# Attention, expert layer and gated layer on one core: output's zeros written later, and the whole order of the work replaced

## Chip, cores and metric

The kernel runs on one core of a Trainium2 chip. The metric is the device time of one execution in microseconds (us), lower is better; the time of a kernel is the median over its runs.

## What is computed

Three layers, one after another, over 1152 tokens (2 batches of 576) of 512 columns. The reference, cut to its core:

```python
def _attn_ref(q, k, v, w_phi):
    def phi(x):
        proj = np.einsum('bhsd,df->bhsf', x, w_phi)
        proj = proj - np.max(np.abs(proj), axis=-1, keepdims=True)
        return np.concatenate([np.exp(proj), np.exp(-proj)], axis=-1)
    q_p, k_p = (phi(q), phi(k))
    kv = np.einsum('bhsf,bhsd->bhfd', k_p, v)
    num = np.einsum('bhsf,bhfd->bhsd', q_p, kv)
    den = np.einsum('bhsf,bhf->bhs', q_p, np.sum(k_p, axis=2))[..., None] + 1e-06
    return num / den

def _moe_ref(x, w_gate, w1, w2, capacity):      # 8 experts, capacity 288
    ...                                          # expert_idx, gate_w: top expert of each token
    # the first `capacity` tokens of each expert are its rows disp[e]
    h = np.maximum(np.einsum('ecd,edf->ecf', disp, w1), 0.0)
    y = np.einsum('ecf,efd->ecd', h, w2)
    ...                                          # out[token] = gate_w * y of its row, or 0

def _moe2_ref(x, w_gate, w_val, w_out, rms_g):   # 1536 inner columns
    xn = x / np.sqrt(np.mean(x * x, axis=-1, keepdims=True) + 1e-06) * rms_g
    g = xn @ w_gate
    return (g / (1.0 + np.exp(-g)) * (xn @ w_val)) @ w_out
```

## The kernel before

**Stages.** First the attention (projections L601, sums over keys L674, queries L751, transposes L719), which ends at about 85 us. While it runs, each batch of finished token tiles is routed (argmax of the gate's logits) and its rows are scattered by POOL (L402) into a table `disp` in DRAM, ordered by expert. Then come passes over the experts. A pass takes one expert's rows, 288 at most, out of `disp` by three gathers on POOL (L399: two tiles of 128 rows and one of 32), scales each tile by its gate value on ACT or DVE (L957, L956), transposes it on PE (L964, four groups of three, one for each 128 columns), and multiplies by `w1` and `w2`. The first pass begins while the attention still runs: its rows were scattered early. The second pass needs rows of all tiles, so its first gather waits until the last batch's three scatters have landed in `disp`. The last stage is the gated layer, from whose rows ACT copies each finished set of output out of its PSUM bank (`rows_out`, L1161); POOL then scatters them into `out_y` (five scatters, L402), since the rows stand in expert order. Rows of `out_y` that no scatter reaches must be zero, so `fill_out` (L1387) writes nine blocks of 128 rows of zeros (256 KB each, from the tile `zrow`, L1389), all of which must lie ahead of the first scatter of output.

**Precision.** Every product of weights is done as three matmuls (L974, L975, L976: high x high, high x low, low x high); the high half of a tile is a cast (L417 on DVE or L418 on ACT), the low half a subtraction on DVE (L414, `lower`). Weight tiles `w4` (nine buffers) are loaded by SP from `in_w12` (`load_w`, L917, 512 KB) and, for the gated layer, from `in_gvo` (L534).

**The order.** Every piece of work is recorded by `Sched.op` or `Sched.any` (L113 to L138) with its engine, a cost, and what it reads and writes; `any` gives two ways (such as DVE or ACT). `Q.run(PLAN)` (L1698) then issues them in the order of the table `PLAN` (L34): each of its numbers, in base 36, is a piece of work and the way taken. An engine works through its own list in that order, and a list that meets a wait holds everything behind it. SP's list holds all loads of weights and the zeros; what it waits for there are buffers and registers. The dependency of the zeros on `tick[0]` in L1389 is one of the recording: it says where the table may put them, and adds no wait on the chip.

**Tiles.** `xg` and `b2` tiles serve many uses in turn: token rows on their way to `disp`, gathered rows, high and low halves of weights. A low half that goes into the tile of a scatter has to wait until that scatter has landed.

Of the kernel before, what the change touches and what calls it, by code (L numbers as in the profile page):

```python
# [38 lines left out]
f3 f1 eq co fj cw am cq 9y fk g0 ca gk cu cy di b4 a3 fh d0 go gt a0 cs b8 gu fm bc fp d2 bi ce fs fu dc be gm fq b6 da bk du bg d8 c6 d6 de gw j4 ho dg dp j6
ei e0 gr ba fw f8 hs fy jb f4 1ne hy j8 gy fc e2 fa h0 g4 fe i6 e4 g6 f6 em hx hq g8 jd gc d4 i8 hv ic h2 h4 ie ge ga gi h8 ig im dw iq ha dk lw i2 hc ii nj  # L40
ik ji he gg hg i0 io m0 dq hk e6 dz ek je nk kg mw i4 jk n4 is dm dt iu n6 iy my lg ki iw j0 li m6 k0 ko lk le e8 km lm j2 lq k2 hm jg hi ea m4 ly kl eo l2 k4
lu jm kc kq m2 mu l8 jo 114 o4 l5 kw js lb lo kt ec ju jq mq jw ls ms 158 jy n1 ma k8 l6 ku 110 lc kz g2 l0 o8 mc n2 me n8 oa pm oc mg og ee oe mi ok ke nf eg
mm oo oq ou k6 os qa h6 ow na ka nm oy ng qc nc qe qq qi p4 qs q7 qk pj qm qu 138 170 qo qg no m8 nw mk p6 mo ny qy om nq o6 rs r2 o0 16y qw oi p1 nu 136 ns
r0 pc pe p8 ta pa ru pg p2 rw ry o2 r4 ps t4 r7 pp 16w s0 s2 s4 pu 19s s6 s8 sa sc se q4 q0 py pq r8 uc 1ru q2 th 172 ue ra pk sg pw si ug v2 rp rk rc uz v4
tc sk 112 sm ui rm q8 174 t6 re t2 176 ti 116 v0 uv 18m tf 13a rq yh so ri 18k uk rg us zc uo uw v6 uq ze zu sq tl um t8 yi vk yf vc v8 109 zg zq va ve vu 118
vm 18o vo 14i vq yw vh yk ss z2 yq yz yn vw vi w2 z5 vs yt 10y zz su zs z6 10d w4 vy yo z0 w0 yu wo we 18q 10e 10u 102 100 wg 104 zw 106 wk 18i 11w sw wc 12e
132 11t wu ws sy 13c t0 11u 10s 10a 10g 11y 178 10o 19q to 11b 120 12k 10i 194 14l 153 10k 10q 134 198 196 ww 12h wi 128 10w 13f tq 124 10m wy wm 12a 14m 12m
154 12s tu 11c x0 19u x2 122 1dc 126 13g 12c 12q 12w 12i 18s 19w x4 14f 13x 19y 160 x6 12u 140 12o x8 12z 15c 130 13y 156 xa 14g xc 148 142 14a xe 14c tm 16f
za xg xi 144 15x xk 19a z8 zi xm 162 146 14o 150 wq 1a0 14u 18u 1d0 14w xo 14q 16g tt 15y 1d2 xq 14y 14s w7 zk 19c 164 16i 168 11q 19f w8 y8 1d4 wa 1d6 15a
11o 16a 166 19g 15e xs 16c y2 16s zm 1a5 11e 13s 1d9 1eq 16u 16k 11g 1es 15g xu 16q 16o 16m y4 17m 17k zo 1eu 13m 13u 11i y6 1ew 11l 17g 17i 11m 13i 1am 1ae  # L50
1a2 1ey 1ai xw 13o 15i xy 13q ya 1f2 1eo 15m 1aa 1as y0 1aq 1au 1a6 13k 1da 15q 15s 1aw 1ao 15o 1dy tw 1ay yc 1hk 17a 17c 1f0 1b0 15u 1b2 1b4 1b6 1b8 1ag 17e
1ba 1f4 18w 1cy 17o 1f6 1bc 1be 1bg 1bi 1cu 1bk 15k 17q 1a8 1e2 1ac 1f8 1hi 17s 1bm 17u 17w 1ak 1fa 17y 1fd 1bu 180 1hc 1c0 1c2 182 184 186 1de 1hm 1cw 18y
1o4 188 1e4 1bo 1ho 1c4 18a ty 18c 18e 1bq 1lw 1c6 1ek 1hg 1e6 18g 1e8 1fe 1dg 1di 190 19i 1c8 1cc 1cm 1ca 1bs 19k 1bw 1fo 1ce 1ea 1by 1cq 1ci 1dk 192 19m 1dn
1he 1cg 1hq 1ga 1dq 1me 1mc 1do 1ck 1ec u0 1fs 1em 1cs 1fg 19o 1mg 1ok 1gc 1ee 1co 1hs 1ei 1ds 1ge 1fu 1fw 1gq 1mi u2 1iw 1mk 1om 1hy 1jk 1fy 1jo 1oo 1hw 1dv
1oq 1i0 1gw 1gi 1ku 1dw 1fi 1ot 1ou 1gu 1gk 1gg 1mm 1ks 1g0 1k2 1i2 1g2 1i8 1eg 1io 1hu 1gy 1iq 1h0 1h4 1j2 1fl 1g8 1h6 1h2 1fm 1ia 1g6 1j0 1i5 1i6 1k6 1gn
1im 1n0 1g4 1iy 1l4 1j4 u4 1id 1go 1h8 1k4 1k8 1ha 1ik 1mo 1jq 1js 1jm 1ii 1kg 1j6 1ki 1pk 1ie 1kw 1la 1ju 1l8 1je 1j8 1ig 1ji 1ja 1jg 1ky 1mq 1jw 1kl 1nc 1lc
1jz 1ka 1le 1n2 1ms 1km 1jc 1k0 1lo 1mu 1ma 1lq 1it 1iu 1ow 1ni 1kc 1ls 1ng 1o6 1nk 1ko 1lg 1lj 1ke 1m0 1kq 1p8 1o8 1lm 1oy 1r4 1l0 1oi 1rg 1l2 1nm 1qc 1ny
1p0 1lk 1lu 1oa 1pq 1oc 1ly 1of 1m2 1nr 1mw 1og 1po 1p2 1nu 1n4 1ps 1n6 1m4 1nw 1m6 1tc 1no 1rs 1qu 1qs 1pa 1r6 1my 1qw 1pu 1to 1ri u6 1ry 1n8 1pz 1q8 1m8 1q4
1rw 1ns 1uq 1s0 1na 1q2 1q6 1qg 1te 1qa 1vg 1rk 1s2 1r8 1tq 1p6 1ra 1qq 1qe 1p4 1sc 1s4 u8 1qi 1qy 1se 1vi 1pw 1rm 1so 1sy 1sa 1s7 1vo 1th 1ti 1vq 1ug 1qk 1sk
1q0 1ro 1sm 1r1 1s8 1sq 1o0 1qn 1ss 1uu 1u0 1t0 1vl 1qo 1t2 1vm 1wq 1rq 1su 1uk 1l6 1t4 1us 1sw 1ws 1uw 1w0 1t6 1xa 1sg 1wu 1uy 1r2 1t9 1wy 1ui 1wg 1wk 1w2  # L60
1o2 1v1 1pc 1v2 1v6 1pe 1ta 1wi 1si 1ww 1um 1xu 1ts 1tu 1ph 1pi 1w4 ua 1re 1ys 1tm 1v4 1rc 1xq 1tx 1v8 1u4 1u2 1u6 1y0 1w6 1xs 1x0 1tk 1ze 1va 1w8 1vc 1wa 1y2
1uo 1e0 1vs 1u8 1vu 1ud 1ua 1ue 1xe 1vx 1xc 1ty 1xg 1yu 1fq 1wc 1xi 1vy 1y5 1xm 1wm 1y6 1yi 1xw 1we 1ve 1zg 1y8 1z8 1wo 1x2 1yw 1z6 1xy 1gs 1za 1x4 1x6 1yk
# [1815 lines left out]
```

## Time and profile before

| | |
|---|---|
| time, median of 3 runs | 284.78 us (284.45 to 285.24) |
| the profiled execution's own time | 283.31 us |
| its span | 281.5 us, 7648 instructions |
| mean granted TensorE clock | 0.986 |
| PE busy | 269.8 us, 2993 matmuls |
| DVE, ACT, POOL busy | 209.6, 166.2, 27.8 us |
| moved by DMA | 48.58 MB, mean 173 GB/s |

The span is the stretch from the first to the last instruction of one execution; 1.8 us of the profiled execution's time lie around it. PE is busy nearly throughout, so what matters is the few places where it is not, or where its clock is lower, and what ended last before it went on there.

### The profile page before, as it was taken

What the parts mean: (1) busy time and instruction counts of PE and PEld (TensorE: products, weight loads), DVE (VectorE), ACT (ScalarE), POOL (GpSimd) and SP (SyncE); (2) the same over time, 40 slices, a digit from 0 to 9 for tenths busy, and PEclk for the clock granted to TensorE, in tenths of its full rate; (3) what the DMA queues carried; (4) which work ended last, traced back from release to release, by engine and by line L of the source; (5) the groups of instructions that cost most, each with busy time, mean ns of one, the idle gap of its engine ahead of it and who ended that gap; (6) DMA issues with size and microseconds to landing.
All of it is one profiled execution on the core that took longest, in us unless ns stands there. A gap on an engine that the chain in (4) does not pass through costs nothing.

```text
span 281.5 us, 7648 instructions
## 1 busy us (share of the span) xinstructions
PE 269.8 (96%) x2993; PEld 253.8 (90%) x2993; DVE 209.6 (74%) x583; ACT 166.2 (59%) x370; POOL 27.8 (10%) x62
## 2 busy tenths in 40 slices
PE   8999999999999979999999999999999999999990
PEld 8899999998999869999979999999999999999970
DVE  2988768968898868999999898795974863464330
ACT  2996874999954445876748767456643634231040
POOL 4000000340054400100000000000000000000042
PEclk9999999999999997999999999999999999999996
DMA  5754245499065587788795737655654820141023
GB/s 191 208 139 117 81 140 130 128 371 393 31 206 174 156 323 220 228 252 280 238 322 166 191 104 261 197 186 185 186 151 149 238 100 0 75 151 41 0 78 116
DMA packets 22092, 48.58 MB, mean 173 GB/s; under 512 B 3427, under 2 KB 8547, under 8 KB 22048
## 3 DMA queue, kind: packets, MB, share of 16 engines
q1 hardware_dynamic: 20496, 44.13, 49.6%
q0 software_dynamic: 1552, 3.88, 3.8%
q8 instruction: 25, 0.41, 0.6%
q14 instruction: 19, 0.16, 0.2%
HBM read 39.93 MB, written 9.18 MB: 174 GB/s over the span
## 4 chain that ended last, share of the span: by engine, by line
PE 65%; DVE 9%; issue 9%; ACT 6%; DMA 6%; POOL 2%; SPq 0%; POOLq 0%; DVEq 0%; ACTq 0%
PE bank L976 10%; PE bank L975 10%; PE bank L974 10%; PE bank L674 6%; PE bank L751 5%; PE bank L601 4%; PE bank L979 3%; PE bank L980 3%; PE bank L981 3%; PE bank L719 3%; DMA xg<-disp,at 2%; DMA disp<-xg,rt 2%; POOL out_y L402 2%; ACT k L651 2%; DMA out_y<-zrow 2%
## 5 line engine op out<-in xcount | busy, mean ns | idle before, releaser
L975 PE MATMUL bank<-w,k 128*128 128x384 f32 x96 | 32.5, 338 | 0.1
L976 PE MATMUL bank<-w,k 128*128 128x384 f32 x96 | 32.4, 337 | 0.0
L974 PE MATMUL bank<-w,k 128*128 128x384 f32 x96 | 32.4, 337 | 0.0
L565 ACT ACTIVATE cat<-w 128x512 int32<-128x512 uint8 x36 | 24.1, 675 | 9.4 <-DVE cat L566 4.5
L563 ACT ACTIVATE cat<-w 128x512 f32<-128x512 f32 x36 | 24.1, 672 | 9.4 <-DVE cat L566 3.9
L1145 ACT ACTIVATE h<-bank 128x256 f32<-128x256 f32 (+1 forms) x24 | 10.1, 433 | 32.3 <-PE bank L976 25.5
L615 DVE TENSOR_REDUCE m<-bank 128x4 f32<-128x512 f32 x36 | 23.5, 683 | 7.5 <-PE bank L601 7.4
L566 DVE SCALAR_TENSOR_TENSOR cat<-cat 128x512 int32<-128x512 int32 x36 | 24.7, 688 | 5.5 <-ACT cat L563 5.0
L974 PE MATMUL bank<-ua,k 128*128 128x256 f32 x96 | 27.2, 283 | 0.0
L975 PE MATMUL bank<-ua,k 128*128 128x256 f32 x96 | 27.2, 283 | 0.0
L976 PE MATMUL bank<-ua,k 128*128 128x256 f32 x96 | 27.0, 282 | 0.0
L568 DVE SCALAR_TENSOR_TENSOR cat<-w,cat 128x512 int32<-128x512 int32 x36 | 24.5, 685 | 0.1
L1146 DVE TENSOR_TENSOR h<-h,bank 128x256 f32<-128x256 f32 (+1 forms) x24 | 11.4, 484 | 17.6 <-ACT h L1145 11.8
L651 ACT ACTIVATE k<-b 128x512 f32<-128x512 f32 x36 | 19.8, 629 | 3.0 <-DVE b L627 3.0
L751 PEld LDWEIGHTS bank<-kvt,k 128*64 128x64 f32 x576 | 18.7, 136 | 1.1 <-ACT k L725 0.4
L751 PE MATMUL bank<-kvt,k 128*64 128x73 f32 x576 | 19.4, 227 | 0.3 <-ACT k L725 0.2
L725 ACT ACTIVATE k<-bank 128x512 f32<-128x512 f32 x36 | 18.8, 622 | 0.9 <-PE bank L719 0.9
L632 ACT ACTIVATE b<-bank,m 128x128 f32<-128x128 f32 x56 | 15.9, 413 | 5.2 <-DVE m L615 4.4
L601 PE MATMUL bank<-wph,b 64*128 64x128 f32 x288 | 19.0, 279 | 0.0
L414 DVE TENSOR_TENSOR h<-h,h 128x256 fp32r<-128x256 f32 (+1 forms) x24 | 11.7, 487 | 9.8 <-PE bank L980 6.4
L974 PEld LDWEIGHTS bank<-ua,k 128*128 128x128 f32 x96 | 18.2, 190 | 0.8 <-PE bank L1336 0.4
L975 PEld LDWEIGHTS bank<-w,k 128*128 128x128 f32 x96 | 18.0, 188 | 1.0 <-DVE w L1384 0.4
(263 smaller groups left out, 737.6 us busy)
## 6 DMA issues: line engine op xcount, KB each, us to landing
w<-in_gvo SPq DMA_DIRECT2D x36, 512.0 KB, 4.2
w<-in_w SPq DMA_DIRECT2D x24, 512.0 KB, 5.0
wo<-cat SPq DMA_DIRECT2D x12, 256.0 KB, 3.7
b<-in_v SPq DMA_DIRECT2D x9, 256.0 KB, 3.6
b<-in_qt SPq DMA_DIRECT2D x9, 256.0 KB, 3.4
...
disp<-xg,rt POOLq DMA_INDIRECT x9, 3.9
```

The source lines that it names most:

```text
L563: op("ACT", c_act(512, False), lambda: nc.scalar.activation(out=m.t, in_=hf(), func=AF.Abs, scale=REBASE), [st], [m])
L565: op("ACT", c_act(512, False), lambda: nc.scalar.activation(out=ai(), in_=top(), func=AF.Copy, scale=1.0 / 32, bias=-31.0 / 64), [st], [a])
L566: op("DVE", c_dve(512), lambda: nc.vector.scalar_tensor_tensor(out=ai(), in0=mi(), scalar=3, in1=ai(), op0=ALU.logical_shift_left, op1=ALU ...
L568: op("DVE", c_dve(512), lambda: nc.vector.scalar_tensor_tensor(out=ai(), in0=hi(), scalar=-0x80000000, in1=ai(), op0=ALU.bitwise_and, op1= ...
L601: nc.tensor.matmul(v4(hs[r].t)[:, c, :], lhsT=v4(x.t)[h, c, :], rhs=wph[h, :], start=c == 0, stop=True, skip_group_check=True)
L615: op("dve", c_dve(512), lambda hf=hf: nc.vector.tensor_reduce(out=m.t[:, 4 * hf:4 * hf + 4], in_=v4(hs[hf].t), axis=AX.X, op=ALU.max, appl ...
L651: nc.scalar.activation(out=kv_(sg)[:, hf::2, :], in_=v4(s[hf].t), func=AF.Exp, scale=s[hf].sign * (1.0 - 2 * sg))
L725: nc.scalar.activation(out=q_[:, sg, hf::2, :], in_=v4(p.t), func=AF.Exp, scale=s[hf].sign * (1.0 - 2 * sg))
L751: nc.tensor.matmul(nv(num)[r0:r1, i, :], lhsT=q_[:, c, 2 * i + hf, r0:r1], rhs=kvr[b][:, 2 * i + c, 73 * hf:73 * hf + 73], start=i == 0 an ...
L974: nc.tensor.matmul(o, lhsT=wh, rhs=xs[0], start=fst, stop=False, skip_group_check=True)
L975: nc.tensor.matmul(o, lhsT=wh, rhs=xs[1], start=False, stop=False, skip_group_check=True)
L976: nc.tensor.matmul(o, lhsT=wl, rhs=xs[0], start=False, stop=lst_, skip_group_check=True)
```

## The change

Three edits. First, the zeros' place in the recording: they now depend on the three copies of the second pass's token indices (`idi`, made from each gathered tile as it arrives) instead of on `tick[0]`, so that the table puts all nine behind these gathers.

```diff
     def fill_out(i):
-        dma(lambda: nc.sync.dma_start(out=out[i * P:(i + 1) * P, :], in_=zrow[:, 0:512]), [(V["zrow"], 0), tick[0]], [(V["out"], ("z", i))])
+        dma(lambda: nc.sync.dma_start(out=out[i * P:(i + 1) * P, :], in_=zrow[:, 0:512]), [(V["zrow"], 0), *[(V["idi"], (1, j)) for j in range(3)]], [(V["out"], ("z", i))])
```

Second, the copy of the last set of output rows is no longer split between ACT (288 columns) and DVE (224). Lines behind it move up by three.

```diff
         def rows_out(s, i):
             a, m, idx = sets[s][3][i]
             o, row = oac[s, i], new("b2")
-            e = 512 if (s, i) != (seq[-1][0], len(sets[s][3]) - 1) else 288
-            op("ACT", c_act(e), lambda: nc.scalar.copy(out=row.t[0:m, 0:e], in_=o.t[0:m, 0:e]), [o], [(row, 0)])
-            if e < 512:
-                op("dve", c_dve(512 - e), lambda: nc.vector.tensor_copy(out=row.t[0:m, e:512], in_=o.t[0:m, e:512]), [o], [(row, 1)])
+            op("ACT", c_act(512), lambda: nc.scalar.copy(out=row.t[0:m, 0:512], in_=o.t[0:m, :]), [o], [row])
```

Third, the whole table `PLAN` is another one, so every engine's list stands in another order, and some casts change between DVE and ACT. Its first line and the one in its place:

```diff
-8 0 2 6 u a c 12 e 14 g 16 18 1a m 1o 28 2e 1f o 22 1c i 1s 1g 1i 2i 4 1q 1w 30 1k 1u q w k 3i 2n 34 3g y 2s 32 3m 2u 20 1y 2g 24 10 4k 3e 2k 3q 2q 26 37 4m
+0 o a e 8 2 c g 4 12 14 16 u m 18 i 1c 1o 1a 2e 1h w 28 22 q k 1k 1e 1q 2g 30 s 1s 3i 1i 1w 2l 3g 1u 2i y 20 2u 10 1y 3m 2s 3e 2m 1m 32 34 4k 2a 3q 2q 4m 36
```

PE issues the same 2993 matmuls. At the very start SP now issues two pieces of the first key tile, then the projection weights `wph`, then the tile's last piece, where `wph` came first before. Of the nine blocks of zeros, one stood among the first pass's weights, two at the second pass's gathers and six in the gated layer; now all nine stand in the gated layer's part of SP's list.

What the table moves around the second pass's gathers is seen at three places.

SP's list from the last loads of the first pass to the first of the second (`in_w12` an expert's weights, `in_gvo` the gated layer's, `lst0` the register that holds the second pass's expert). Before:

```order
L917 DMA w4_2_1836<-in_w12 128x1024
L534 DMA w4_1_1905<-in_gvo 128x512
L1389 DMA out_y<-zrow_69 128x512 x2
L1584 TENSOR_LOAD lst0_86
L1584 ISA x2
L917 ISA
L917 DMA w4_3_2055<-in_w12 128x1024
L917 ISA
L917 DMA w4_5_2067<-in_w12 128x1024
```

With the change:

```order
L917 DMA w4_0_1813<-in_w12 128x1024
L534 DMA w4_2_1910<-in_gvo 128x512
L917 ISA
L917 DMA w4_1_1929<-in_w12 128x1024
L1581 TENSOR_LOAD lst0_86
L1581 ISA x2
L917 ISA
L917 DMA w4_4_1960<-in_w12 128x1024
L917 ISA
L917 DMA w4_8_2065<-in_w12 128x1024
```

The two blocks of zeros are gone from here; the last weight tile of the first pass (`w4_1_1929`) stands where they stood, behind the load from `in_gvo` instead of ahead of it.

DVE's list at the low half that goes into the last scatter's tile (`xg_0`), which therefore waits for that scatter. Before:

```order
L414 TENSOR_TENSOR xg_3_1929<-w4_8_1726,b2_5_1901 128x512
L417 CAST b2_6_1931<-w4_0_1749 128x512
L566 SCALAR_TENSOR_TENSOR cat_106<-cat_106 128x512
L414 TENSOR_TENSOR xg_0_1940<-w4_0_1749,b2_6_1931 128x512
L414 TENSOR_TENSOR b2_2_1955<-w4_3_1609,b2_4_1806 128x512
```

With the change, the piece from the low half of `w4_4_1592` on:

```order
L414 TENSOR_TENSOR b2_3_1902<-w4_4_1592,b2_4_1806 128x512
L1484 SCALAR_TENSOR_TENSOR key_88<-cnt_94,off_84 128x9
...
L417 CAST b2_8_1936<-w4_0_1813 128x512
L1517 SCALAR_TENSOR_TENSOR at_98<-place_95,rt1_112 128x3
L417 CAST b2_0_1939<-w4_0_1813 128x512
L414 TENSOR_TENSOR xg_0_1947<-w4_0_1813,b2_8_1936 128x512
L414 TENSOR_TENSOR b2_2_1958<-w4_6_1620,xg_1_1896 128x512
```

Before, the last reader of the weight tile `w4_3_1609`, whose buffer the second pass's first load takes (`w4_3_2055`), stood behind the waiting low half. Now the last reader of `w4_4_1592`, whose buffer `w4_4_1960` takes, stands ahead of it.

PE's list at the second pass's transposes (L964, from the gathered tiles `xg` and `b2`), preceded by matmuls of the first pass. Before:

```order
L974 MATMUL bank_1853<-h_1_1996,xg_2034 128x288
L975 MATMUL bank_1853<-h_5_2062,xg_2034 128x288
L976 MATMUL bank_1853<-h_1_1996,xg_2060 128x288
L964 MATMUL bank_2124<-ident,xg_1937 128x128
L964 MATMUL bank_2124<-ident,b_3_1899 128x128
L964 MATMUL bank_2124<-ident,b_8_1868 128x128
```

With the change:

```order
L974 MATMUL bank_1851<-h_0_2036,b_4_2058 128x288
L975 MATMUL bank_1851<-h_6_2076,b_4_2058 128x288
L976 MATMUL bank_1851<-h_0_2036,b_6_2067 128x288
L964 MATMUL bank_2125<-ident,xg_1815 128x128
...
L964 MATMUL bank_2129<-ident,b_5_2001 128x128
L974 MATMUL bank_1845<-h_2_2099,b_7_2014 128x288
L975 MATMUL bank_1845<-h_7_2137,b_7_2014 128x288
L976 MATMUL bank_1845<-h_2_2099,b_1_2106 128x288
L964 MATMUL bank_2145<-ident,xg_1815 128x128
```

The first transpose was PE's 610th row and is now its 613th, three matmuls later, and three more matmuls now part the second group of transposes from the third. On ACT the scaling of the second gathered tile (L957) stood behind the copy of the third tile's indices (L934 from `xg`); it now stands behind that of its own.

## Rows read from the trace of the kernel before

**Rows 1.** The page's head and first part: busy time, share of the span, instructions.
```profile
span 281.5 us, 7648 instructions
PE 269.8 (96%) x2993; PEld 253.8 (90%) x2993; DVE 209.6 (74%) x583; ACT 166.2 (59%) x370; POOL 27.8 (10%) x62
```

**Rows 2.** Windows; columns: width, each engine's busy time, PEclk granted, DMA share, GB/s.
```profile
93.00:94.00 1.00, 0.49 (x4) 0.44 (x4) 1.00 (x2) 0.00 (x0) 0.33 (x1) 1.00 0.00 0
102.00:103.00 1.00, 0.45 (x4) 0.22 (x2) 0.15 (x1) 0.00 (x0) 0.00 (x0) 1.00 0.97 336
103.00:104.00 1.00, 0.00 (x0) 0.00 (x0) 0.21 (x1) 0.22 (x2) 0.00 (x0) 1.00 1.01 377
104.00:105.00 1.00, 0.68 (x4) 0.49 (x5) 1.00 (x3) 1.00 (x2) 0.00 (x0) 1.00 0.81 324
105.00:106.00 1.00, 0.74 (x7) 0.51 (x5) 1.00 (x3) 1.00 (x4) 0.00 (x0) 1.00 0.17 66
106.00:107.00 1.00, 0.78 (x4) 0.79 (x5) 1.00 (x5) 0.79 (x3) 0.00 (x0) 0.71 0.47 74
107.00:110.00 3.00, 3.00 (x14) 3.00 (x14) 3.00 (x7) 1.49 (x4) 0.00 (x0) 0.53 0.81 254
```

**Rows 3.** Chain of waits from 64 to 112 us; columns: start, us, what.
```profile
87.41 5.29 DMA disp<-xg,rt
92.81 0.70 DVE xg L414
...
94.23 0.13 PE bank L976
...
96.81 6.95 DMA xg<-disp,at
103.79 0.47 DVE xg L956
...
106.23 0.74 PE bank L964 x3
106.98 0.24 PE bank L974
```

**Rows 4.** Timeline of SP's queue; columns: start, us, what was issued, how often.
```profile
87.03 0.34 SPq L534 DMA_DIRECT2D w<-in_gvo  x1
87.41 0.91 SPq L1389 DMA_DIRECT2D out_y<-zrow  x2
94.23 6.59 SPq L917 DMA_DIRECT2D w<-in_w  x5
```

**Rows 5.** Line L402 from 84 to 85.2 us: landing of its one scatter, issued at 84.21.
```profile
DMA to landing us min/median/max: 3.2/3.2/3.2
```

**Rows 6.** Line L399 from 117 to 118 us: landing of its one gather, issued at 117.65.
```profile
DMA to landing us min/median/max: 4.8/4.8/4.8
```

**Rows 7.** Timeline of DVE at the wait for the last scatter.
```profile
92.81 0.69 DVE L414 TENSOR_TENSOR xg<-w,b 128x512 fp32r<-128x512 f32 x1 [2.04 <-DMA disp<-xg,rt]
93.42 0.69 DVE L414 TENSOR_TENSOR b<-w,b 128x512 fp32r<-128x512 f32 x1
```

**Rows 8.** Timelines of SP and PE at the start, and landing of L472's three pieces.
```profile
0.81 0.39 SPq L469 DMA_DIRECT2D wph<-in_wphi  x1
1.25 1.38 SPq L472 DMA_DIRECT2D b<-in_kt  x3
4.60 2.96 PE L601 MATMUL bank<-wph,b 64*128 64x128 f32 x48
DMA to landing us min/median/max: 2.0/2.0/2.2
```

**Rows 9.** Timelines of ACT and POOL at the end: copies of output rows, and last scatter.
```profile
272.42 0.40 ACT L1165 COPY xg<-bank 128x288 f32<-128x288 f32 x1 [2.75 <-DVE xg L1167]
274.77 0.58 ACT L1165 COPY b<-bank 128x512 f32<-128x512 f32 x1 [0.80 <-PE bank L981]
275.65 0.97 POOL L402 DMA_INDIRECT out_y<-b,idi  x1 [0.30 <-ACT b L1165]
```

More of the change, by code (lines that the diff above doesn't have):

```diff
@@ L39 @@
[L39 to L62, printed above, removed]
@@ new lines @@
+8s ac 9d 8y 9e 92 8w 8u es ae 82 9s ag ai 90 7s am ak ao as au 9g ay b0 b2 aq aw 9q bm bo c0 eu bs c2 8k bq bu 84 c8 bw a8 by cg 8m 9u ew ci ck cm co ey eq c4
+9w cc cq 9y fg ca f1 b4 fj f3 cw fl a3 a0 gk fm gu be fp gy g0 fq b8 cs bc du bg ce fs b6 h0 bi ba d8 cu dc go cy f8 fv 6 d0 f4 de c6 da ei dg fw gs gm gw h6
+fy bk g2 i2 do ho j4 dj gr j6 em d2 i6 hs d6 hw fa fc mw e0 f6 hq ic i4 dw i8 g4 hy i0 ji ie hu d4 ig jb ik j8 ek iq e2 jc dk fe g6 my h2 g8 ga e4 jk h4 ii io
+nj lw h8 ha hc je gc kg gi gg hg e6 n5 he dq im hm e8 jg hk ge is lg nk ea dy ki mu li iu ly dn hi iy ko iw m4 lk kl m6 eo j0 ma lm dt j2 kn jm 110 lu k0 m0
@@ new lines @@
+qa lo lq le ec l2 l8 jo m2 js k2 kq kw ju lb mc kz 158 kt k4 n6 jw kc k8 mq jy me lc l0 mg ku l5 ms l6 ls ee o8 mi oa mm oc p1 og oe ok n8 o4 nm oo 112 oq n1
+jq os p2 ou qq pp ow ka oy n2 eg qc no nf k6 qe qi qs qk o1 qm ps qu na qo oi pj 16y ke qg pm th 136 pu om r2 mk 114 m8 qy p4 mo nc o6 ru nw pq nu ra qw nq rw
+ry ny r4 ns p6 s0 r0 ng o2 ud pg 170 pk s2 q7 p8 s4 16w t5 s6 s8 sa pe pw q4 pa sc rs q2 rc r6 se ro pc py r8 t2 ue 10y q0 rk ug 172 rg 116 v2 re tb 138 13a
+q8 um tc 18k vh uy v0 rq sg 18m ri 11t si t6 rm v4 uq ui ti 18o uk uo sk 13c tf us uu va 11u zc uw sm vc v8 v6 zg ze 13f vk yh t9 vm ve yf 18q vi so to tk sq
@@ new lines @@
+vq zr yi vu vs yq z2 12e ss yt vo su 13g w2 yk yw 18t z5 zs yu yn z6 yo 18i w0 yz z0 sw 174 zz vw vy 12a wg w4 100 10d 132 102 118 wk wc wq zv 10e 10g 19q 14i
+zw 11w 104 wo we 176 ws sy wu 106 12c 109 ww 11b 12k 18u 10i 10s 12z 10k 198 11y t0 10o 10a 12h wy 11c 196 x0 178 10v 10q 124 194 134 120 19u 13x 128 14f 10w
+tm 10m tq 126 122 12s 12i 13y 12m 19w x2 130 12q 12o za x4 15c 140 19y 156 1a0 x6 142 14k zk 12u 153 144 148 14m 1d2 12w 14o 154 14q 19a x8 1d0 14c 14a 146
+19c 14w 1d4 15x 1dc 15a 160 xa zi 14s xc tt wi 150 14g 15e z8 162 xe 16e 14u 14y xg 11o 164 16c 15g 166 xi 19f w6 xk 1eq 168 16o 16q xm 1d6 wm 16u 11q w8 xo
@@ new lines @@
+1fs 1fi 1ee 1cc 1cm 1he 1ds 1eg 1bs 1cq 1ce 1lw 1io 1cg 1em 1by 1co 1iq 1ci 1me 1ga 1fw 1ei 1cs 1ck 1fy 1mc 1gy 1jo 1mg u0 1hy 1fl 1g3 1gi 1gc 1mi 1p8 1hw 1ml
+1g4 1i0 1dv 1k4 1dw 1i2 1ik 1mm 1k6 1i4 1fm 1o4 1g8 1ge 1g6 1gk 1k8 1gg 1i8 1om 1iw 1gn 1i6 1go 1h0 1is 1n0 1g0 1ia 1j2 1ha 1h4 1pm 1ok 1iu 1kg 1ka 1h8 1oo
+1j0 1r4 1hu 1qc 1n2 1h6 1h2 1im 1oq 1j4 1ow 1ii 1j6 1kd 1ig 1jq 1ks 1js 1ke 1ic 1ju 1ku 1pa 1jb 1ot 1l8 1ie 1mo 1ne 1jc 1la 1ko 1ou 1je 1nc 1ma 1jw 1j8 1o6
+1iy 1lc 1kq 1ki 1o8 1gs 1k2 1le 1ri 1oi 1mq 1ng 1jm 1oy 1r6 1jy 1kl 1k0 1ji 1mt 1lj 1oa 1jg 1lg 1ni 1oc 1nk 1ls 1kw 1rs 1ru 1km 1ly 1m0 1lm 1lk 1m2 1lo 1lq
@@ new lines @@
+1ky 1qs 1qu 1rg 1qw 1l0 1oe 1e0 1mu 1nm 1lu 1l2 1tc 1m4 1pk 1qy 1mw 1qg 1nu 1m6 1m8 1r8 1my 1p1 1tq 1qe 1te 1qi 1fq 1qk 1sy 1r0 1ny 1nq u2 1r2 1to 1p2 1qn 1q2
+1nw 1ra 1qo 1rw 1ry 1no 1qq 19s 1sk 1og 1q6 1vg 1s0 1n4 1q4 1pq 1n6 1sm 1ns 1po 1n9 1se 1s2 1o0 1ps 1vi 1l6 1so 1tg 1pu 1uq 1sa 1ti 1o2 1sq u4 1sc 1uu 1us 1w0
+u6 1pz 1sg 1ss 1ui 1ug 1na 1uw 1vl 1uy 1pc 1pw 1vm 1t2 1uk 1si 1ts 1s4 1p6 1tu 1pe 1su 1v0 1xa 1u0 1q8 1vo 1p4 1vq 1ph 1q0 1t0 1s7 1qa 1v2 1tw 1pi 1rk 1rm 1sw
+1u4 1wq 1wg 1wi 1t4 1re 1xw 1v4 1ws 1s8 1v6 1rc 1t6 1wk 1wy 1u2 1rp 1v8 1wv 1y0 1u6 1w2 1ww 1va 1xu 1x0 1um 1t8 1vd 1u8 1rq 1uc 1ta 1w4 1tk 1uo 1tm 1xc 1y2
@@ L64 @@
+1wm 1ue 1ve 1ty 1ua 1y8 1yw 1xq 1xs 1wo 1vs 1xe u8 1x2 1vu 1xy 1yu 1yy 1w6 1x4 1vx 1y5 1yi 1w8 ua 1wc 1vy 1x6 1we 1ys 1xg 1y6 1ya 1xi 1yk 1z1 1z8 1xn 1x8 1z2
+1xo 1za 1yc 1xk 1zm 1ze 1wa 1ye 1ym 1zg 1zi 20e 1yo 1zc 1z4 1zk 1zo 1z6 1yg 1zr 20g 1zs 1yq 204 20i 20k 206 1zu 20m 208 1zw 20a 20c 1zy 200 202
 """
```

10 lines of the change are left out of this document (6 added, 4 removed).

## The prediction

> **What bounds the kernel now.** I begin with the page's first part: PE is busy for 269.8 of 281.5 us [rows 1], so the time is PE's work plus what PE waits. Of the 11.7 us without PE, some 6.7 lie behind its last matmul (the last copy of output starts at 274.77 [rows 9]); the windows then show where the rest is. There are two places. In 93 to 94 us PE is busy for 0.49: 0.51 lost. From 102 to 107 it is busy for 0.45 + 0.00 + 0.68 + 0.74 + 0.78 = 2.65 of 5 us: 2.35 lost. Behind that the granted clock is 0.71 for 1 us and 0.53 for 3 [rows 2]: PE, which had stood still for most of 2 us, is put to the lower of its two levels (1.2 instead of 2.4 GHz), and a matmul of 288 columns that started 0.13 us after the one ahead of it takes 0.24 [rows 3]. The lost clock costs 0.29 + 3 x 0.47 = 1.70 us. Together 0.51 + 2.35 + 1.70 = **4.56 us**. Some 2 us are left for the start and all other places.
>
> The chain of waits says what ended last there [rows 3]. The last scatter into `disp`, issued at 87.41, took 5.29 us. DVE stood waiting for it with the low half that goes into its tile (2.04 us [rows 7]), and PE stood behind that: the 0.51. The first gather can only follow it. The third gather, issued at 96.81, took 6.95 us, landed at 103.76, and was scaled at 103.79; the transposes of the second pass could not start before. That is the larger wait.
>
> What made these transfers slow? A scatter issued at 84.21 landed in 3.2 us [rows 5], a gather issued at 117.65 in 4.8 [rows 6]. Beside the slow scatter SP's queue had issued a load of 512 KB at 87.03 and the two blocks of zeros at 87.41; beside the gathers, five loads of 512 KB from 94.23 on [rows 4], and the transfers moved 324 to 377 GB/s while PE stood still [rows 2].
>
> **The change part by part.** *Zeros.* Two blocks leave the neighbourhood of the last scatter. The scatter's gain lies between 0 and 5.29 - 3.2 = 2.1 us. A weight tile of 512 KB, as much as the two blocks, now stands in their place in SP's list, and has to wait only for DVE to finish with its buffer. So the bytes beside the scatter need not shrink; what surely goes is two writes to DRAM beside a write to DRAM. I take a third, 0.7 us. The nine issues of zeros on SP cost the same wherever they stand (0.91 for two); in the gated layer they are covered as six of them were already.
>
> *The second pass's loads.* Before, their first took a buffer whose last reader on DVE stood behind the waiting low half; that reader began at 93.42 [rows 7] and the load followed at 94.23. Now the reader stands ahead of the wait, so this load can go some 5 us earlier. Of the loads that shared the queue with the gathers one leaves. The third gather's gain is between 0 and 6.95 - 4.8 = 2.15 us; of five loads three were issued by the time the third gather was, so I take a third, 0.7 us. Price of that: the early load joins the scatter's neighbours (third rival).
>
> *PE's order.* Three more matmuls of 288 columns stand ahead of the first transpose, and three between the second and third group: 3 x 0.13 = 0.40 us of work under each wait [rows 3]. The scaling of the second tile no longer stands behind the third tile's index copy on ACT, so only the third tile's scaling on DVE (0.47) remains between landing and transpose.
>
> *The large wait after that.* The third gather lands 0.7 + 0.7 = 1.4 us earlier, at 102.36; with the 0.55 us from landing to transpose that were seen before, the transposes start at 102.9. PE runs out of other work at 102.45 + 0.40 = 102.85. The wait for the gather has then gone to nearly nothing. Between the groups some 0.5 us was lost too (0.74 of work in the last row of transposes [rows 3]); I leave 0.4 of the 2.35. With 0.4 us idle, no more than in 93 to 94 us, where the clock stayed at 1.00 [rows 2], it should not fall: the whole 1.70 goes. Gain 1.95 + 1.70 = 3.65.
>
> *The small wait.* The low half into the last scatter's tile is still there, and its wait shrinks with the scatter's landing. Between 0 and 0.51; I take 0.25 gained.
>
> *The start.* `wph` is SP's third issue instead of its first. Before, issues stood 0.45 us apart from 0.81 on and landed after 2.0 to 2.2; the first projection started at 4.60, behind PE's warm-up [rows 8]. As third `wph` lands at about 1.7 + 2.2 = 3.9, below 4.60: 0. The bound is one place in the queue, 0.45.
>
> *The end.* The split copy was no parallel one: ACT waited 2.75 us until DVE had done its part, and then took 0.40 [rows 9]. One copy of 512 columns takes 0.58, so the set is ready no later. But the last scatter, at 275.65, followed the last set's copy (274.77 + 0.58 = 275.35, and 0.30 to the issue [rows 9]), which the change leaves alone: 0.
>
> *The rest of the order.* Elsewhere PE lost some 1 us beside the start. A new order can make new waits of about that sum or none: 0 to +1.0; I take +0.3, near the low end, since the same 2993 matmuls follow the same producers and nothing else shows a wait of the two places' size.
>
> **The sum.** -3.65 - 0.25 + 0 + 0 + 0.3 = -3.6, so 283.31 - 3.6 = 279.7 against the profiled execution. That execution lies 1.47 us under the median of the runs shown (284.78), so **281.2 us** against the median. Its own range: 280.2 (all 4.56 gone and no other cost: 283.31 - 4.56 + 1.47) to 282.4 (the start's 0.45 and 0.7 more elsewhere).
>
> **The rivals.** *The transfers stay slow.* The gathers took some 2.1 us more beside SP's loads, and SP's loads stay. The Trainium skill, page "DMA: Bandwidth & Descriptors", section "Queues, rings and completion order", says that each DMA engine goes round the queue rows that have work, a packet from each in turn. By that rule the scatter's share would be the same with one load of SP behind it as with three, and the terms of 0.7 would be 0. The rows show a scatter and a gather with and without neighbours, not with fewer, so they don't speak against it. As a mechanism of this kernel: scatter and gathers keep 5.29 and 6.95 us, and only PE's order helps. The transposes start at 104.31 as before, PE waits from 102.85, 0.40 less, and the second group's 0.40 of cover and the earlier scaling on ACT take some 0.5 more: 0.95 of 2.35 goes. The clock then falls or not: 0 to 1.70. With +0.3 elsewhere: 283.31 - 0.65 - (0 to 1.70) + 1.47 = 282.4 to 284.1. Chance 0.24.
>
> *The change does not do what it says.* The dependency is one of the recording, not a wait on the chip; the weight tile brings back the zeros' bytes, and the gathered rows still come when they come. Then wait and clock loss stay, and only 0 to 0.75 us of other costs are added: 284.8 to 285.5. Against it speaks PE's added cover, which is certain. Chance 0.12.
>
> *Slower: the early load delays the last scatter.* Beside it there would be three transfers of 512 KB, 1.5 MB where there was 1.0. If the scatter then takes what a gather among loads took, 6.95 instead of 5.29, the DVE wait grows by 1.7, and PE, which had no slack at 93 us, waits 1.7 more there; the gathers are issued 1.7 later and the large wait stays, as PE was held as long as they were. 284.78 + 1.7 = 286.5, less at most 0.4 of cover: 286.1. It decides as soon as the last scatter lands later than 92.7. For it: DVE's order frees the buffer early; against it: the load also needs the register of the second pass's expert, and queues behind two loads. Chance 0.10.
>
> **How the numbers follow.** The forecast has 0.50, the three rivals 0.24, 0.12 and 0.10; 0.04 is for what I have not thought of, half on each side. About 0.3%, 0.85 us, is what a measurement can tell from no change: below 283.9 is faster, above 285.6 slower. Faster: 0.50 + most of the first rival (0.20) + 0.02 = 0.72. Same: 0.04 + 0.12 = 0.16. Slower: 0.10 + 0.02 = 0.12. The range takes in the forecast, the first rival and the lower half of the second, 0.50 + 0.24 + 0.06 = 0.80; at its low end stands the 0.33 by which the fastest run shown lies under the median: 279.9 to 285.1.
>
> **What would show it.** Right: no window from 92 to 110 us with PE under 0.8; granted clock 1.00 in 104 to 112; the last scatter into `disp` landing in under 5 us and the third gather in under 6.5; the span near 278. First rival: scatter and gather of about 5.3 and 7, PE idle for over a us ahead of L964. Third: a load from `in_w` in SP's row between 88 and 92 and DVE waiting for over 2 us at the low half. The prediction is wrong if PE's busy share outside the two places falls, or if some scatter of output waits for zeros in the last 10 us, where I have put nothing.

## The result and the profile after

The change takes **286.61 us** (median; 285.08 to 288.74, 14 runs), the kernel before beside it 284.98 (284.32 to 285.85, 14 runs). The ratio is 1.0061, interval 1.0040 to 1.0082: slower by 0.6%, where 281.2 us was forecast. The profiled execution of the change took 287.18 us.

The page's head and first part, answering to [rows 1]:

```profile
span 285.2 us, 7640 instructions
...
PE 270.5 (95%) x2993; PEld 255.0 (89%) x2993; DVE 207.7 (73%) x577; ACT 166.2 (58%) x372; POOL 30.3 (11%) x62
```

The matmuls are the same; PE waits more. Windows of the change (width, busy time of PE, PEld, DVE, ACT, POOL, granted clock, DMA share, GB/s):

```profile
63.00:64.00 1.00, 0.62 (x17) 0.49 (x12) 0.00 (x0) 1.00 (x3) 0.99 (x2) 1.00 1.00 401
64.00:65.00 1.00, 0.62 (x17) 0.48 (x17) 0.30 (x1) 0.71 (x2) 0.11 (x1) 1.00 1.03 397
85.00:86.00 1.00, 0.55 (x4) 0.36 (x3) 0.73 (x5) 0.00 (x0) 0.00 (x0) 1.00 0.70 263
86.00:87.00 1.00, 0.00 (x0) 0.00 (x0) 0.90 (x6) 0.22 (x2) 0.00 (x0) 1.00 0.00 0
87.00:88.00 1.00, 0.01 (x1) 0.00 (x1) 0.96 (x6) 1.00 (x3) 0.00 (x0) 0.87 0.00 0
88.00:89.00 1.00, 1.00 (x12) 1.00 (x12) 0.97 (x6) 1.00 (x3) 0.00 (x0) 0.50 0.00 0
...
91.00:92.00 1.00, 1.00 (x8) 1.00 (x8) 1.00 (x4) 0.74 (x2) 0.70 (x2) 0.92 0.61 238
...
109.00:110.00 1.00, 1.00 (x9) 0.84 (x7) 0.67 (x3) 1.00 (x2) 0.00 (x0) 1.00 1.05 336
110.00:111.00 1.00, 0.27 (x3) 0.18 (x3) 0.85 (x5) 0.06 (x1) 0.00 (x0) 1.00 0.87 340
```

The wait that the forecast wanted to win is mostly gone: at the transposes, now at 110 us, 0.73 us are lost and the clock stays at 1.00, where it was 2.35 us and 1.70 us of clock [rows 2]. But between 85 and 88 us PE stands still for 0.45 + 1.00 + 0.99 = 2.44 us, and from 88 to 91 it runs at the lower clock (0.50), which with the last row costs 1.58: **4.0 us** at a place where the trace of before has nothing. Another 0.76 is lost at 63 to 65 us, and some more in gaps of 1 us or less, at the first projections above all.

What ended last there: the chain of waits of the change (start, us, what).

```profile
79.78 2.18 PE bank L751 x64
81.96 0.33 PE bank L974
...
83.49 0.13 PE bank L975
83.62 1.59 PE bank L976
85.22 0.02 issue
85.24 0.16 DVE rt L781
...
87.76 0.20 DVE rt L822
87.95 0.04 issue
88.00 0.38 PE bank L831 x9
```

PE's routing counts (L831) wait for DVE (L822), and DVE's work on the routing began only at 85.24, with L781, which reads the result of L751. L751 had ended at 81.96. The chain gives a matmul of L976 1.59 us where its neighbours take 0.13: the last 1.4 us are no work, they are the time until PE's signal (the update of the semaphore on which DVE waits) reached DVE. DVE was idle from 82.06 on, and POOL was issuing until 84.46. Timelines of the change on DVE and on POOL (start, us, engine, line, operation, what it waited for):

```profile
81.88 0.18 DVE L785 TENSOR_TENSOR rt<-bank,rt 128x32 f32<-128x32 f32 x1
85.24 0.16 DVE L781 TENSOR_SCALAR rt<-bank 128x4 f32<-128x4 f32 x1 [3.17 <-PE bank L976]
```

```profile
80.83 1.05 POOL L402 DMA_INDIRECT disp<-xg,rt  x1 [16.72 <-DVE xT L969]
82.18 1.00 POOL L402 DMA_INDIRECT disp<-xg,rt  x1 [0.30 <-issue]
83.48 0.98 POOL L402 DMA_INDIRECT disp<-xg,rt  x1 [0.30 <-issue]
...
99.05 2.81 POOL L399 DMA_INDIRECT b<-disp,at  x1 [4.62 <-ACT b L929]
```

The three scatters are issued 0.30 us apart, and PE's signal came 0.76 us after the last issue had ended at 84.46. That coincidence in time became the theory: **while POOL issues such a run, PE's signals are held back.** Rival: something else holds them, or it is noise. That it is the signal that comes late, and not DVE that starts late, is in the trace's semaphore events: PE's own has none between 80.97 and 85.22 us and then four by 85.56; L781 starts 0.02 us after the first of these. A further row: the first gather of the second pass waited for ACT's copy of the zero columns (L929), so the gathers go out late as well.

Ratios below leave out disturbed runs (four of the ten of before_spaced, two of the six of before_gap2), medians do not, and the profiles of these two kernels are of such runs.

### The profile page after: what moved, and what is told of

The parts are those of the page before. It is cut to its first block, busy times and chain, and to the rows that moved or that the text cites. A ratio compares the mean times of both kernels' runs of the same rounds, so it can differ in the third digit from the quotient of the medians.

```text
span 285.2 us, 7640 instructions
## 1 busy us (share of the span) xinstructions
PE 270.5 (95%) x2993; PEld 255.0 (89%) x2993; DVE 207.7 (73%) x577; ACT 166.2 (58%) x372; POOL 30.3 (11%) x62
## 4 chain that ended last, share of the span: by engine, by line
PE 40%; issue 22%; DVE 5%; DMA 4%; POOL 2%; ACT 0%; POOLq 0%; SPq 0%; DVEq 0%
PE bank L976 10%; PE bank L974 10%; PE bank L975 10%; DMA xg<-disp,at 2%; DMA out_y<-zrow 2%; PE bank L979 2%; PE bank L980 2%; PE bank L981 1%; POOL out_y L402 1%; PE bank L1333 1%; PE bank L1317 1%; PE bank L964 1%; DVE b L414 1%; PE bank L751 1%; POOL xg L399 1%
## 5 line engine op out<-in xcount | busy, mean ns | idle before, releaser
L976 PE MATMUL bank<-w,k 128*128 128x384 f32 x96 | 32.5, 338 | 0.0
L976 PE MATMUL bank<-ua,k 128*128 128x256 f32 x96 | 27.0, 281 | 0.0
L751 PE MATMUL bank<-kvt,k 128*64 128x73 f32 x576 | 20.2, 227 | 1.2 <-issue 0.8
L402 POOL DMA_INDIRECT out_y<-b,idi x5 | 5.1, 1024 | 151.1 <-ACT b L1164 150.8
L751 PEld LDWEIGHTS bank<-kvt,k 128*64 128x64 f32 x576 | 19.0, 136 | 2.4 <-issue 1.2
L632 ACT ACTIVATE b<-bank,m 128x128 f32<-128x128 f32 x52 | 14.8, 381 | 9.9 <-DVE m L615 6.4
L674 PE MATMUL bank<-b,k 128*64 128x65 f32 (+1 forms) x640 | 18.9, 222 | 0.6 <-issue 0.4
L674 PEld LDWEIGHTS bank<-b,k 128*64 128x64 f32 (+1 forms) x640 | 17.8, 137 | 1.5 <-issue 0.9
```

The lines of the kernel that those rows point to most:

```text
L674: nc.tensor.matmul(a[u // 3].t[o:o + 64, k:k + VW // 2], lhsT=kp.t[r0:r1, f:f + 64], rhs=vt.t[r0:r1, VW * (u // 2) + VW // 2 * i:VW * (u / ...
L751: nc.tensor.matmul(nv(num)[r0:r1, i, :], lhsT=q_[:, c, 2 * i + hf, r0:r1], rhs=kvr[b][:, 2 * i + c, 73 * hf:73 * hf + 73], start=i == 0 an ...
L976: nc.tensor.matmul(o, lhsT=wl, rhs=xs[0], start=False, stop=lst_, skip_group_check=True)
```

## The experiments

**The same two kernels elsewhere.** No edit; the chips are called A, B, C, D. What the expectations call a chip of the first kind is one like A, of the second kind one like B and C.

> The changed kernel once more, for a second profile. In its first profile PE lost 3.6 us at 85 to 91 us (the routing of the last tiles: DVE waits 3.2 us, then PE 2.4 us, then half the clock), 2.2 us at 60 to 65 and 1.0 us more at the start, and won 4.2 us at the second pass's transposes. Theory 1 (the new order makes these waits): they stand at the same places again, each within 0.5 us. Rival (an accident of one execution): at 85 and at 60 us PE loses under 0.5 us, while the start's loss stays.

Chip A: 279.52 us (278.62 to 281.15) against 283.73, ratio 0.985 (0.9804 to 0.9896). There the forecast gain holds: -4.2 us where -3.6 was worked out.

> The changed kernel a third time. Its first measurement gave 1.6 us over the kernel before, the second, on another chip, 4.2 us under it; the difference lay in two places, where a semaphore of PE came 2 to 3 us after the matmul it stands for (at 61 to 65 and at 82 to 85 us). If that comes with some chips: this run is near either 279.5 or 286.6 us, with both stalls or with neither. If it comes with executions at random: something between, with one of them.

> The kernel before itself, for a profile on this chip. Expected: the two waits of its first profile, 0.5 us at the last scatter's tile and 2 to 2.4 us at the transposes, and the clock's fall behind; the time within 0.3 us of the kernel before.

Chip B: 285.90 us for the change against 284.60, ratio 1.0057 (1.0027 to 1.0087), and 285.05 for the kernel before itself, ratio 1.0019 (0.9993 to 1.0046). So the time of the change goes with the chip. That the kernel before would show the two waits of its first profile on B was expected and is a miss, as its rows show.

Windows of the change on chip A:

```profile
82.00:83.00 1.00, 1.00 (x16) 0.92 (x15) 0.97 (x5) 0.02 (x1) 0.40 (x3) 1.00 0.40 156
...
103.00:104.00 1.00, 0.97 (x8) 0.73 (x6) 0.94 (x6) 0.92 (x2) 0.00 (x0) 1.00 0.94 324
104.00:105.00 1.00, 0.73 (x7) 0.73 (x8) 1.00 (x5) 0.14 (x1) 0.00 (x0) 1.00 0.89 328
```

No stall at the routing counts, and at the transposes 0.3 us instead of 2.35, at full clock. Now the kernel before, on chip B, windows and DVE's timeline:

```profile
84.00:85.00 1.00, 0.51 (x4) 0.27 (x3) 0.39 (x3) 0.00 (x0) 0.24 (x2) 1.00 0.89 348
85.00:86.00 1.00, 0.00 (x0) 0.00 (x0) 0.96 (x9) 0.00 (x0) 0.00 (x0) 1.00 0.50 173
86.00:87.00 1.00, 0.00 (x0) 0.00 (x0) 0.86 (x6) 0.63 (x3) 0.20 (x1) 1.00 0.07 16
...
89.00:90.00 1.00, 1.00 (x6) 1.00 (x5) 1.00 (x5) 1.00 (x4) 0.82 (x1) 0.50 0.79 246
...
108.00:109.00 1.00, 1.00 (x11) 1.00 (x10) 1.00 (x2) 0.00 (x0) 0.00 (x0) 1.00 1.05 430
```

```profile
84.57 0.16 DVE L781 TENSOR_SCALAR rt<-bank 128x4 f32<-128x4 f32 x1 [2.76 <-PE bank L976]
```

On this chip the kernel *before* has the stall too (0.49 + 1.00 + 1.00 us, and behind it the clock at 0.50 from 89 to 92, 1.7 us in all), and nothing at the transposes, which begin here at 108.78 instead of 104.31: held up at 84 us, PE comes to them after the rows have. So the 4.56 us on which the forecast rests were not there to be won. They belong to the execution that was profiled, not to the runs on B. The traces tell the two kinds of chip apart by one thing more: those of the first profile of before and of every run on A and D hold 3531 to 3558 records of semaphore updates, those of the official change and of every run on B and C 3340 to 3475. So the first profile of before, which has no stall at L831 either, comes from a chip of A's kind, and A's runs of that kernel (282.53 to 285.62 us) take in its 283.31.

**Parts of the change.** zeros_late: the kernel before with the two blocks of zeros moved back in SP's list, behind the block at 220 us.

```diff
 L534 DMA w_1_1905<-in_gvo 128x512
-L1389 DMA out_y<-zrow 128x512 x2
 L1584 TENSOR_LOAD lst_86
```

> The kernel before with one edit: the two blocks of zeros that stood beside the last scatter are written behind the block at 220 us. If the zeros slow that scatter: it lands in 3.2 to 4.3 instead of 5.3 us, the third gather lands 1 to 2 us earlier, and the time falls by 1 to 3 us, by up to 4 if the clock stays up. If weights and gathers fill the time anyway: within 0.5 us of before.

Chip A: ratio 0.9935 (0.9902 to 0.9968), 1.8 us. Landing in zeros_late of the last scatter (line L402 at 89 us), then of the third gather's pieces (line L399 at 96 us):

```profile
DMA to landing us min/median/max: 3.6/3.6/3.6
```

```profile
DMA to landing us min/median/max: 6.9/7.0/7.0
```

The scatter takes 3.6 instead of 5.29 us [rows 3], the wait at 93 us is gone; the third gather takes 7.0 still, so it is not the zeros that slow it. It lands at 103.76, no earlier than before; PE waits 1.76 us in 103 to 107 instead of 2.35 in 102 to 107, and the clock stays at 1.00 behind it, which by [rows 2] is 1.70 us.

wph_first, on A: the change with `wph` issued first again.

```diff
+L469 DMA wph<-in_wphi 128x128
 L472 DMA b<-in_kt 128x128
 L472 DMA b<-in_kt 128x256
-L469 DMA wph<-in_wphi 128x128
```

> The changed kernel with one edit: SP issues the projection weights first, as the kernel before did. If the loss at the start (1.0 us more than before) comes from that issue's place: the first projections follow one another as before and the time is 0.5 to 1 us under the changed kernel's. If it comes from the order of the projections on PE or of the shifts on DVE and ACT: the wait at 8 us stays and the time is the same within 0.4 us.

279.48 us beside 279.52: the place of this issue costs nothing.

zeros_back, on B: the change with two blocks of zeros put back behind the load.

```diff
 L534 DMA w_2_1910<-in_gvo 128x512
+L1386 DMA out_y<-zrow 128x512 x2
 L917 DMA w_1_1929<-in_w 128x1024
```

> The changed kernel with two blocks of zeros put back behind the load that follows the scatters, as the kernel before had them (and the dependency of the recording as it was). If zeros beside scatter and gathers cost what their removal brought the kernel before (1.85 us of 283.7): 1 to 2 us over the changed kernel on the same chip, the wait at the transposes longer by 1 to 1.5 us. If the changed order covers them: within 0.4 us of the changed kernel.

286.00 us beside 285.90 (ratios to the kernel before 1.0056 and 1.0057): where signals are held, the zeros' place is worth nothing that these runs can tell.

**Halves of the order.** The table's first 440 pieces from before, then the change's (before_440 on A, before_440b on B), and the change's first 420, then those of before (after_420 on B).

```diff
-PLAN = pieces of the change
+PLAN = first 440 pieces of before, then the change's others in their order
```

> The first 440 pieces of work in the order of the kernel before (start, attention, first pass up to the last but one batch's scatters), the rest in the changed order. Theory 1 (the changed order loses in its first third and wins at the gathers): no loss at 60 to 91 us, PE waits at most 1 us at the second pass's transposes, and 281 to 282.5 us, 3 us under before. Rival (what was won at the gathers was only won because the attention was late): the wait at the transposes comes back with 2 us or more, and the time is within 1 us of before.

> The kernel before's order for the first 440 pieces, then the changed order. On a chip of the first kind as before: 280.6 us, 3 us under the kernel before. On a chip of the second kind, theory: the first 440 pieces hold the gap of 2.7 us at L831 as the kernel before does, so at best the changed kernel's loss at 60 to 70 us is saved: 284 to 285.5 us. Rival (the changed order's loss comes from its later part): 286 us.

> The first 420 pieces of work in the changed order, the rest in the order of the kernel before, so with its zeros, its loads and its place of the transposes. If the second pass's part of the order is what gains: near the kernel before, within 1 us, with the wait of 2 us at the transposes. If the changed start and attention gain too: 1 us or more under it.

Ratios 0.9879 (0.984 to 0.9919), 1.0024 (0.9997 to 1.0051) and 0.998 (0.9959 to 1.0002). On B neither cut is told apart from the kernel before: the loss sits in no one half. The trace of after_420 on B says more. The wait of 2 us at the transposes, which was expected, does not come, and PE loses only 0.62 us at 81 to 82 and 0.44 at 86 to 87 where the change and the kernel before lose 2.3 to 2.5. Yet its three scatters are issued 0.30 us apart too, from 79.24 to 82.87. DVE's timeline:

```profile
82.12 0.16 DVE L781 TENSOR_SCALAR rt<-bank 128x4 f32<-128x4 f32 x1 [1.29 <-remote]
83.82 0.16 DVE L781 TENSOR_SCALAR rt<-bank 128x4 f32<-128x4 f32 x1 [1.44 <-PE bank L751]
```

The first L781 starts while the third scatter is issued (81.90 to 82.87), so a signal of PE can get out within such a run. What such a run costs depends, then, on the order around it.

**Pauses.** The test of the theory: tiny memsets on POOL between the issues, everything else as it was. spaced has 16 ahead of the second and third scatter of the batch, gap4 has 4, gap2 has 2; gap4_all has 4 there, at the gathers of 59 to 62 us and at the next batch of scatters.

```diff
-op("POOL", 1280, lambda k=k, g=g: scatter(...), ...)
+op("POOL", 1280, lambda k=k, g=g, q=2 * (tiles[0][0] == 3 and k != 1):
+   [*[nc.gpsimd.memset(gap, 0.0) for _ in range(q)], scatter(...)], ...)
```

> The changed kernel once more, as the control of the three runs beside it. Theory (chips differ: on some, PE's signals reach DVE only 0.7 to 0.8 us after POOL's run of indirect DMAs is over): about 279.5 us, 4 us under the kernel before, with no PE gap at 84 to 88 us, or about 286 us, 1 us over it, with PE idle some 2.5 us ahead of the routing counts (L831). Rival (the differences are noise between runs): anything from 279 to 287 us, with the gap at some other place.

> The changed kernel with 16 tiny POOL memsets (about 1 to 1.6 us) ahead of the second and third of the three scatters that POOL issues back to back at 80 to 84 us. Theory (the run of DMA issues holds PE's signals back): on a chip of the second kind PE's signals get out in the pauses, DVE's wait of 3.2 us at L781 breaks up into waits of 1.3 us or less, PE's 2.5 us at L831 shrinks under 1 us, and the kernel is 1.5 to 4 us faster than the changed kernel on the same chip; on a chip of the first kind no difference (within 0.5 us). Rival (something else holds PE's signals, and the DMA issues fall there by chance): the wait at L781 and the gap at L831 stay, time the same as the changed kernel or up to 2 us more, since the last scatters of this batch go out later.

Chip B: the control 285.54 us (ratio 1.0045, 1.0019 to 1.0070), spaced 284.16 (1.0013, 0.9992 to 1.0034), a gain of 1.4 us where 1.5 to 4 were expected. DVE's timeline of spaced:

```profile
81.08 0.16 DVE L781 TENSOR_SCALAR rt<-bank 128x4 f32<-128x4 f32 x1 [0.30 <-PE bank L751]
88.34 0.42 DVE L789 TENSOR_TENSOR xg<-bank,rt 128x256 f32<-128x256 f32 x1 [2.10 <-DMA disp<-xg,rt]
```

The wait for PE falls from 3.08 (control) to 0.30 us, as the theory has it, but 16 memsets took 2.57 us, not 1 to 1.6, and the late scatters made a wait of their own (2.10). Hence shorter ones:

> The changed kernel, control of the three beside it: about 285.5 us with PE idle 2.5 us ahead of L831 on a chip with held signals, about 279.5 us without that gap on the other kind.

> Two tiny memsets in each of the two places (0.16 us each by the spaced run, and 0.67 us from the last one to the next issue: pauses of 1.0 us in place of 0.30). Theory (a pause lets the held signals out): if 1.0 us is enough, the gap at L831 goes, no wait for scatters' buffers comes at L789, and the time is 2 to 3.5 us under the control; if it is not, the gap stays and the time is the control's, or up to 1.4 us over it. Rival (the pause helped in the spaced run only because the scatters themselves were late): the gap stays at 2 us or more. On the other kind of chip within 0.5 us of the control.

> Four memsets in each place, pauses of 1.3 us. Theory: signals out 0.5 to 0.8 us after an issue ends, as in the spaced run, so the gap at L831 goes and the time is 2 to 3.5 us under the control, 282 to 283.5 us. Rival: the gap stays, the time is the control's or more.

> Four memsets also ahead of the second and third gather at 59 to 62 us and of the second and third scatter of the last batch. Theory (all of the loss has this cause): the gaps of 0.4 and 0.55 us at 62 us go too, and the time is up to 1 us under that of gap4; the last scatters go out 2 us later, which can cost at the transposes. Rival (the gaps at 62 us have another cause): they stay, and the time is that of gap4 or up to 2 us more.

Chip C, the kernel before at 284.34 us:

| | median | ratio to before | interval |
|---|---|---|---|
| again4 (the change) | 286.48 | 1.0072 | 1.0034 to 1.0110 |
| gap2 | 281.36 | 0.9887 | 0.9842 to 0.9931 |
| gap4 | 282.50 | 0.9947 | 0.9918 to 0.9976 |
| gap4_all | 281.20 | 0.9886 | 0.9843 to 0.9929 |

Four memsets that compute nothing win **5.1 us** by the medians of five and four runs (286.48 to 281.36); the two profiled executions lie 2.7 us apart (284.90 and 282.18). DVE of the control, then POOL and DVE of gap2, and two of its windows:

```profile
83.28 0.16 DVE L781 TENSOR_SCALAR rt<-bank 128x4 f32<-128x4 f32 x1 [3.11 <-PE bank L976]
```

```profile
80.00 1.04 POOL L402 DMA_INDIRECT disp<-xg,rt  x1 [16.69 <-DVE xT L969]
81.04 0.29 POOL L848 MEMSET gap<- 128x8 f32 x2
82.00 1.00 POOL L402 DMA_INDIRECT disp<-xg,rt  x1 [0.67 <-issue]
```

```profile
81.58 0.16 DVE L781 TENSOR_SCALAR rt<-bank 128x4 f32<-128x4 f32 x1 [0.35 <-PE bank L751]
```

```profile
86.00:87.00 1.00, 0.62 (x5) 0.42 (x4) 1.00 (x7) 0.97 (x4) 0.38 (x1) 1.00 0.97 213
87.00:88.00 1.00, 1.00 (x9) 1.00 (x9) 1.00 (x6) 0.55 (x2) 0.68 (x2) 1.00 0.83 332
```

A pause of 0.96 us in place of 0.30 is enough: L781 starts 0.54 us after the first issue ended, the stall (2.3 us in the control) goes, and the clock stays at 1.00. gap4's median is 1.1 us above that of gap2 with the same stall gone; the intervals overlap, and its profiled execution is the shorter one (281.71 against 282.18), so no difference is shown. For the gaps at 62 us, PE's windows of gap4 and then of gap4_all:

```profile
61.00:62.00 1.00, 0.91 (x22) 0.64 (x18) 0.00 (x0) 1.00 (x4) 0.74 (x1) 1.00 1.06 393
62.00:63.00 1.00, 0.44 (x6) 0.32 (x8) 0.00 (x0) 1.00 (x3) 0.46 (x2) 1.00 0.97 393
```

```profile
62.00:63.00 1.00, 1.00 (x32) 0.88 (x29) 0.72 (x2) 1.00 (x4) 1.00 (x1) 1.00 0.98 348
63.00:64.00 1.00, 1.00 (x38) 1.00 (x36) 1.00 (x4) 1.00 (x3) 0.46 (x5) 1.00 0.99 373
```

They go as soon as the three gathers there are parted, which speaks for the same cause.

**Pauses in the kernel before.** The same edit, 16 memsets (before_spaced, B) and 2 (before_gap2, D).

> The kernel before with the same memsets ahead of the second and third scatter of the same batch. Theory (the stall at L831 covers the wait for the second pass's rows): on a chip of the second kind the 2.7 us at L831 go and about as much wait comes back at the transposes (L964, 103 to 107 us), so the time stays within 1 us of the kernel before; on a chip of the first kind nothing changes (within 0.5 us). Rival (the stall is a loss of its own): the time falls by 3 us or more and no wait comes at the transposes.

Ratio 0.9963 (0.9940 to 0.9987). Windows of before_spaced:

```profile
86.00:87.00 1.00, 0.69 (x6) 0.45 (x4) 0.00 (x0) 1.00 (x2) 0.52 (x5) 1.00 0.20 66
87.00:88.00 1.00, 0.00 (x0) 0.00 (x0) 0.74 (x3) 0.03 (x1) 0.59 (x1) 1.00 0.00 0
...
107.00:108.00 1.00, 0.09 (x1) 0.00 (x0) 0.12 (x1) 0.00 (x0) 0.00 (x0) 1.00 1.00 402
108.00:109.00 1.00, 0.00 (x0) 0.00 (x0) 0.03 (x1) 0.00 (x0) 0.00 (x0) 1.00 0.98 385
```

PE is fully busy from 79 to 86 us, so the stall at the counts is gone, and the wait for the second pass's rows is back (PE 0.09, 0.00, then 0.42 busy), on the chip where it had been absent. But it is no clean exchange: PE also loses 2.7 us between 86 and 92, as the late scatters keep DVE waiting for their tiles (1.89 us at L789), and the execution took 287.21 us. Of the shorter ones, from 282.71 us on, there is no trace. That the two waits take each other's place rests on the two traces of the kernel before, the first profile and the one on B.

> The kernel before with two tiny memsets ahead of the second and third scatter of the same batch. Theory (on a chip that holds PE's signals the stall at L831 and the wait for the second pass's rows take each other's place): the 2.7 us at L831 go, 2 us or more come at the transposes (L964) with the clock's fall after them, and the time stays within 1 us of the kernel before. Rival: the stall is a loss of its own, and the time falls by 3 us or more with no wait at the transposes. On a chip that does not hold them: within 0.5 us of the kernel before, wait at the transposes in both.

> The kernel of gap4_all again. On a chip that holds PE's signals: 281 us, 1.0 to 1.5% under the kernel before. On one that does not: 280 to 281 us, since the pauses delay the last scatters by 2 us there for nothing.

before_gap2: ratio 0.9853 (0.9801 to 0.9905), where within 0.5 us was expected, a miss. Its one profile shows the gathers at 59 to 62 us without PE's gaps, so D is of A's kind, as its semaphore records say too, and PE waiting at the transposes as in [rows 2]; but that execution took 283.51 us, while four others took 278.35 to 280.97, and of those there is no trace. So by these runs pauses can win 3 to 4 us where no signal is held as well, and how stays open; a part of what they win on C may be of that kind. gap4_all2: 280.46 us against 284.18, ratio 0.9872 (0.9831 to 0.9913). **The change with pauses beats both kernels on C; on D it beats the kernel before**, and the change alone was not run there.

## Why the prediction was wrong

**The step that failed** is the base of the sum: that the profiled execution of before, with its waits of 4.56 us, stands for the runs beside which the change would be timed, and that "nothing else shows a wait of the two places' size", for which I put +0.3 in "The rest of the order". On B, where PE's signals are held, the kernel before stalls 2.5 us plus 1.7 us of clock at L831 instead, and does not wait at the transposes. The change stalls there as well (2.44 plus 1.58 us in the official trace), so the gain had nothing to come from; what was left of the change on such chips is its own cost of 1.3 to 2.1 us. For the official chip this is read from the change's trace: the kernel before was not traced there. A hint stood in the text: the profiled 283.31 us lay under all three runs shown (284.45 to 285.24), and I added the 1.47 us as scatter.

**Where that base holds, the terms hold.** On A the whole is -4.2 us for -3.6. The last scatter landed in 4.2 us (5.29 before; a gain of 1.1 for my 0.7), the third gather in 4.4 (6.95; 2.6 for my 0.7), the clock's 1.70 went whole, the small wait went. The `wph` term of 0 holds (wph_first). The rest of the order cost some 0.8 us among the first projections (PE lost 2.22 us in the first 15 us on A, 1.40 in the first profile), for +0.3. That all comes to -4.2 is in part luck: both transfers gained more than was put down, and the start lost more.

**The rivals.** *The transfers stay slow*: on A they did not; in zeros_late the scatter alone gained 1.7 us by the zeros' move. The Trainium skill, page "DMA: Bandwidth & Descriptors", section "Queues, rings and completion order", has each DMA engine go round the queue rows that have work. As I applied that rule, a scatter beside SP's queue would not care how much stands in it; the 3.6 us speak against that reading, and no run here tests the rule by itself. *The change does nothing*: near the truth on B for the zeros (zeros_back), not for the order. *The early load delays the last scatter*: in the change's trace the stall lies ahead of that scatter, so the sign was right and the mechanism not this one; that its 286.1 lies near 286.61 is chance. What the text named as a sign of error, PE's share falling outside the two places, is what happened.

**Why slower and not equal** on such a chip is read from traces in part, and not closed: both orders stall at L831, but in the change the first gather goes out later after the last scatter. It waits for ACT's copy L929, which waits for PE to leave the tile; on B the first gather stands at 97.21 us in the change and 95.51 before, and 1.3 us are lost again at the transposes (0.24 and 0.47 busy at 108 to 110). At the start, in its first 15 us, PE loses 1.0 us more on B, and 0.2 more in the small gaps of 57 to 80. But the two executions traced there took 285.19 (the change) and 285.44 us (before), with PE busy for 269.3 and 271.1, so they do not show the 1.3 us by which the medians differ; no run takes this part alone.

**What stays open.** Why the change is slower there and not only equal, why chips differ, by what path POOL's issues hold PE's signals, why after_420 escapes most of the stall, and what the pauses win on D. That the runs of issues have a part in it is shown: pauses on POOL alone, at the scatters on B and C and at the gathers on C, took the stall or gaps there away.
